# Loads of the values' matrices in the line of q and k, and three groups of early scores at other units, in a top-k attention with MLP

## The chip, the core and the metric

The kernel runs on one core of a Trainium2 chip. The metric is the device time of one execution in microseconds (us), as the median of several. A profile is one execution, recorded instruction by instruction; its span runs from the first instruction to the last.

Names: PE is TensorE (PEld its weight loads), DVE is VectorE, ACT is ScalarE, POOL is GpSimd, SP is SyncE, which issues every DMA of this kernel in the order of the program.

## The reference

Attention over 8 batches of 8 heads, 576 queries and keys, 64 dimensions a head, in float32. Of each row of scores the 32 largest are kept, and a softmax runs over them; then an MLP with 2048 hidden channels over the 4608 tokens.

```python
scores = scale * np.matmul(q, k.transpose(0, 1, 3, 2))
kth = np.partition(scores, -top_k, axis=-1)[..., -top_k:-top_k + 1]
scores = np.where(scores >= kth, scores, -1000000000.0)
attn = np.exp(scores - np.max(scores, axis=-1, keepdims=True))
attn = attn / (np.sum(attn, axis=-1, keepdims=True) + 1e-09)
x = np.matmul(attn, v)   # then (4608, 512), heads side by side
h = x @ w_in
out = np.maximum(0.01 * h, h) @ w_out
```

## The kernel before, in words

**Units.** Two heads form a pair: 32 pairs, four to a batch. A unit is 128 queries of a pair (or 64 queries of each of two pairs, for what is left of 576 = 4 x 128 + 64). There are 18 units to a batch, 144 in all, worked through one to a step: `cur = unit(s)` in step s. In even batches the 16 whole units come first and the two left ones last; in odd batches the left ones come first. So pairs 4 to 7 (batch 1) belong to units 18 to 35, pairs 8 to 11 to units 36 to 53, and so on.

**A unit's way.** Each step handles four units at different stages.

- Scores (`scores`, lines 203 to 237): in every even step PE computes the scores of units s + 2 and s + 3 as a pair into PSUM, and ACT copies them to SBUF (`s_sb`, line 235).
- Top-k of unit s (`top_k`): DVE runs four rounds of MAX8 (line 304) and MATCH_REPLACE8 (line 307) on larger and smaller halves (`pairs`, line 299).
- Unit s - 1: POOL masks (`pen`, lines 317 and 318), ACT takes exponents and their sums (line 321), then `ze` (line 326).
- Unit s - 2: DVE takes the reciprocals `rz` of `ze` (line 330), ACT normalizes (line 333). ACT then splits the words in two halves (`split`, line 342), each is written to DRAM (`apart`, line 343, 288 KB), and one transposing DMA reads both back (`wT`, line 347). Units 14, 15, 23 and 31 (`HASTY`) are transposed on PE instead (lines 357 and 363).
- Values: units n - 1 and n (n odd, from 15 on) are due together at the end of step n + 3 (`values_at`; one step earlier for n = 15, 23 and 31). There PE multiplies wT of the two units with the values' matrices `vt` (line 386, for left units line 398), and ACT copies the result to `x` (line 410).

**The MLP.** When all units of a chunk of 256 tokens have their values, its matmuls (`ph`, line 455, and `pz`, line 467) are dealt out in slots between these parts by a budget (`slot_budget`): the backlog spread over the slots up to the step that brings the next chunk.

**Loads.** q and k of a pair (`qt`, `kt`, eight pairs held, two 288 KB transfers a pair) wait in a list `waiting` and are issued one transfer a step, right after a unit's transposing DMA (line 671). The values' matrices (`vt`, five held, one 320 KB transfer a pair) are issued by `load_more` at the end of a step, as soon as the pair five before was last used four steps ago, several at once if they are due.

**Early scores.** The scores of twelve whole units are computed in steps 0 to 5 and put into DRAM (`keep_scores`, 576 KB a unit). `KEPT` names three groups a; a group is units a, a + 1, a + 8 and a + 9. Three steps ahead of its top-k such a unit's scores are fetched (`s_sb<-kept`, line 290, 576 KB), at the place where otherwise a transfer of the list goes. In the even step that would have computed the pair nothing is computed:

```python
            if unit(s + 3) in early_units:
                fetch_scores(unit(s + 3))
            elif waiting:
                nc.sync.dma_start(*waiting.pop(0))
...
            if new and new[0] in early_units:
                new = ()
```

The order within each engine is the order of the program; nothing is moved by a scheduler. In the functions below the line numbers are those of the profile.

Of the kernel before, what the change touches and what calls it, by code (L numbers as in the profile page):

```python
# [20 lines left out]
def kernel(  # L21
# [13 lines left out]
    nc = tc.nc  # L35
    NPAIR, P, S = qT.shape
# [20 lines left out]
    LOADED, LOADED_V = 5, 5  # L57
# [102 lines left out]
    qk_of, v_of = {}, {}  # L160

    def load_qk(pi, at_once=True):
        if pi % (LOADED + 3) < LOADED:
            qt = loads.tile([P, S], F32, name="qt")
            kt = loads.tile([P, S], F32, name="kt")
        else:
            raw = raws.tile([P, WCH, 4], U16, name="raw").rearrange("p n w -> p (n w)").bitcast(F32)
            qt, kt = raw[:, 0:S], raw[:, S:2 * S]
        waiting.extend([(qt, qT[pi]), (kt, kT[pi])])
        qk_of[pi] = qt, kt  # L170
        if at_once:
            while waiting:
                nc.sync.dma_start(*waiting.pop(0))

    waiting = []

    def load_v(pi):
        v_of[pi] = loads.tile([P, NKC, 2, D], F32, name="vt", bufs=LOADED_V)
        nc.sync.dma_start(v_of[pi], vk[pi])

    class Unit:

# [71 lines left out]
    def load_early(us):  # L254

        raw = raws.tile([P, WCH, 4], U16, name="raw").rearrange("p n w -> p (n w)").bitcast(F32)
        at = 0
        for pi in sorted({u.pairs[0] for u in us}):
            kt = raw[:, at:at + S]
            nc.sync.dma_start(kt, kT[pi])  # L260
            at += S
            for u in us:
                if u.pairs[0] == pi:
                    early_of[u] = raw[:, at:at + P], kt
                    nc.sync.dma_start(early_of[u][0], qT[pi][:, u.q0:u.q0 + P])
                    at += P
# [61 lines left out]
    def reciprocals(u):  # L328
        u.rz = small.tile([P, 2], F32, name="rz")
        nc.vector.reciprocal(u.rz, u.ze)  # L330
# [175 lines left out]
    LAG = 3  # L506
# [6 lines left out]
    def values_at(n):  # L513

        if n < UNHURRIED:
            return (n | 1) + LAG + 1, MIDDLE
        return (n | 1) + LAG - ((n | 1) in HURRIED), END

    steps = units

    KEPT = (24, 40, 56)
    EARLY_SCORES = {0: 4, 1: 2, 2: 1, 3: 2, 4: 1, 5: 2}

    def unit(n):
# [26 lines left out]

    with tc.manual_schedule():
        last = {p: n for n, u in enumerate(steps) for p in u.pairs}

        to_keep = [[steps[n] for n in (a, a + 1, a + 8, a + 9)] for a in KEPT]
        early_units = {u for us in to_keep for u in us}
        to_load, to_keep = list(to_keep), [u for us in to_keep for u in us]
        assert all(len(u.pairs) == 1 for u in to_keep)

        def score_early(count):  # L560

            for _ in range(min(count, len(to_keep))):
                keep_scores(to_keep.pop(0))
                if len(to_keep) % 4 == 0 and to_load:
                    load_early(to_load.pop(0))

        def load_more(s):

            for of, load, n, lag in ((v_of, load_v, LOADED_V, LAG + 1), (qk_of, load_qk, LOADED + 3, 8)):
                if of is qk_of and to_keep:  # L570
                    while len(of) < LOADED:
                        load(len(of))
                    continue
                while len(of) < NPAIR and (len(of) < n or last[len(of) - n] + lag <= s):
                    if of is v_of or len(of) < n:
                        load(len(of))
                    else:
                        if not waiting:
                            load(len(of), at_once=False)
                        break  # L580


        for n in range(3):
            load_weights(n)
        jobs = [round_weights(*job) for job in ROUNDED] if AS_WORDS else [iter(())] * len(ROUNDED)
        for n in range(len(jobs) + 1):
            if n == len(jobs) - 1:
                first = first_scores(steps[0])
                next(first, None)
            for job in jobs[max(n - 1, 0):n + 1][::-1]:  # L590
                next(job, None)
            if n == len(jobs) - 1:
                next(first, None)
                load_v(0)
                load_v(1)
            elif n == len(jobs):
                for _ in first_scores(steps[1]):
                    pass
            if n:
                load_weights(n + 2)  # L600
            if n >= len(jobs) - 2:
                load_early(to_load.pop(0))
            if 0 <= n - len(jobs) + HP + 1 < HP:
                load_qk(n - len(jobs) + HP + 1)

        def weights_of(u):
            reciprocals(u)
            normalize(u, 0)
            normalize(u, 1)

        def values(*place):
            due = [u for n, u in enumerate(steps) if values_at(n) == place]
            if not due:
                return ()
            po = ps_sc.tile([P, 2, 512], F32, name="wide", bufs=2)
            if len(due[0].pairs) == 1:
                weigh_whole(due, po, FULL + [NKC - 1] if place[1] == MIDDLE else
                            [QUARTERS] + FULL if place[0] < HURRY else FULL + [QUARTERS])
                return [(due[0], po[:, :, 0:P])]
            for n, u in enumerate(due):  # L620
                weigh_left(u, po[:, :, n * LEFT:(n + 1) * LEFT])
            return [(u, po[:, :, n * LEFT:(n + 1) * LEFT]) for n, u in enumerate(due)]

        def keep(weighed, *place):
            for u, po in weighed:
                keep_values(u.pairs[0], po, u.b, u.q0)
            attended(*place)

        for s in range(len(steps) + LAG + 1):
            assert s < 7 or not to_keep  # L630
            cur, old, older, new = unit(s), unit(s - 1), unit(s - 2), ()
            if s % 2 == 0:
                new = [u for u in steps[s + 2:s + 4] if u]
            picks = top_k(cur) if cur else iter(())
            budget = slot_budget(s)

            def slot():
                next(picks, None)

            at_first = s < HURRY and s - 2 in HURRIED  # L640
            if at_first:
                weights_of(older)
            slot()
            if old:
                mask(old, 0)
                mask(old, 1)
            late = s < HURRY and not {s - 1, s - 2} & set(HURRIED)
            if older and not late and not at_first:
                weights_of(older)
            mlp_steps(budget)  # L650
            weighed = values(s, MIDDLE)
            at_once = s - 2 in HASTY or any(at == (s, MIDDLE) for at, _ in ready_at)
            if at_once:
                keep(weighed, s, MIDDLE)
            slot()
            if older and late:
                weights_of(older)
            if s - 2 in HASTY:
                transpose_in_haste(older)
            mlp_steps(budget)  # L660
            if old:
                exponents(old, 0)
            mlp_steps(budget)
            if older:
                keep_transposed(older) if s - 2 in HASTY else transpose(older, lambda: mlp_steps(budget))
            if not older or s - 2 in HASTY:
                mlp_steps(budget)
            if unit(s + 3) in early_units:
                fetch_scores(unit(s + 3))
            elif waiting:  # L670
                nc.sync.dma_start(*waiting.pop(0))
            slot()
            slot()
            mlp_steps(budget)
            if old:
                exponents(old, 1)
                sums(old)
            mlp_steps(budget)
            if not at_once:
                keep(weighed, s, MIDDLE)  # L680
            if new and new[0] in early_units:
                new = ()
            if new and s < HURRY:
                scores(new)
            keep(values(s, END), s, END)
            if new and s >= HURRY:
                scores(new)
            score_early(EARLY_SCORES.get(s, 0))
            budget = slot_budget(s + 1)
            mlp_steps(budget)  # L690
            load_more(s)
        mlp_steps(1e9)

# [58 lines left out]
```

## Time and profile before

| | |
|---|---|
| median of 3 runs | 1460.74 us (1458.87 to 1461.27) |
| the profiled execution | 1460.92 us, of it span 1458.9 us |
| mean TensorE clock granted | 0.983 |
| PE busy | 1397.0 us, 96% of the span |
| PEld busy | 904.6 us, 62% |
| DVE busy | 1319.8 us, 90% |
| ACT busy | 1101.0 us, 75% |
| POOL busy | 1096.4 us, 75% |

The first top-k begins at 60.7 us, that of unit 143 at 1363.2 us. What follows after about 1384 us is MLP on PE. PE's busy time counts a matmul from its start to a modelled end, and overlapping ones once. A stage's PEclk is the share of the full TensorE clock that was granted. An engine's idle time is put down to what ended it ("<-"); a wait that does not hold up the end costs nothing.

### The profile page before, as it was taken

To read this page: it belongs to the slowest core of one execution; us is meant where nothing else is said; L and a number is where in the kernel's file an instruction comes from. 1 tells how busy PE (TensorE), PEld (TensorE's weight loads), DVE (VectorE), ACT (ScalarE), POOL (GpSimd) and SP (SyncE) were. 2 spreads that over 40 slices of the span, in tenths; PEclk is the share of its full clock that TensorE was granted. 3 is DMA by queue.
4 is the path that set the end of the run, shared out by engine and by line. 5 is a ranking of instruction groups with operands and counts; after the bars stand their busy time and mean duration, and the time that the engine had idled before them with its cause. 6 is when DMAs were issued, how large, how long until landed. Compare 5 with 4: busy or idle time off the path is not lost.

```text
span 1458.9 us, 26037 instructions
## 1 busy us (share of the span) xinstructions
PE 1397.0 (96%) x8978; PEld 904.6 (62%) x8980; DVE 1319.8 (90%) x3401; ACT 1101.0 (75%) x1984; POOL 1096.4 (75%) x744
## 2 busy tenths in 40 slices
PE   7848999899989999999999999999999999999998
PEld 2324548475656666666666666666666666666674
DVE  7999999989999999999999999999999999999600
ACT  8878888577767777778787878787878787778710
POOL 3388888878887888888888888888888888788600
PEclk9968999999999999999999999999999999999999
DMA  9967544647476676667666655557555665554610
GB/s 334 338 213 228 140 119 117 185 117 185 137 192 170 179 173 161 187 167 191 169 158 165 176 145 139 166 156 177 148 161 163 171 155 130 171 138 128 154 40 14
DMA packets 394996, 239.14 MB, mean 164 GB/s; under 512 B 334576, under 2 KB 336112, under 8 KB 392944
## 3 DMA queue, kind: packets, MB, share of 16 engines
q1 hardware_dynamic: 394864, 237.48, 58.7%
q8 instruction: 70, 1.15, 0.3%
q14 instruction: 62, 0.51, 0.1%
HBM read 55.77 MB, written 99.09 MB: 106 GB/s over the span
## 4 chain that ended last, share of the span: by engine, by line
PE 74%; DVE 12%; DMA 7%; ACT 5%; issue 1%; SPq 0%; POOL 0%; DVEq 0%; ACTq 0%; POOLq 0%
PE ph L455 28%; PE pz L467 28%; PE wide L386 9%; DVE tops L304 5%; PE wide L228 4%; DVE pairs L307 4%; DMA apart<-split 3%; PE narrow L228 3%; DMA wT<-apart 3%; ACT split L342 2%; DVE pairs L299 1%; PE wide L398 1%; ACT s_sb L321 1%; ACT s_sb L333 1%; DMA raw<-in_weights_dram 1%
## 5 line engine op out<-in xcount | busy, mean ns | idle before, releaser
L317 POOL TENSOR_SCALAR pen<-s_sb,tops 128x576 f32<-128x576 f32 x288 | 637.5, 2213 | 202.0 <-DVE tops L304 130.0
L304 DVE MAX8 tops<-pairs 128x8 f32<-128x288 f32 (+1 forms) x1152 | 636.0, 591 | 0.0
L467 PE MATMUL pz<-w_out,gT 128*128 128x512 f32 x1152 | 504.7, 594 | 2.4 <-ACT scale L428 2.4
L455 PE MATMUL ph<-x,w_in 128*128 128x256 f32 x2176 | 482.6, 381 | 0.0
L307 DVE MATCH_REPLACE8 pairs<-tops,pairs 128x288 f32<-128x288 f32 (+1 forms) x864 | 460.3, 538 | 0.0
L455 PEld LDWEIGHTS ph<-x,w_in 128*128 128x128 f32 x2176 | 409.5, 190 | 77.3 <-issue 23.1
L318 POOL TENSOR_TENSOR s_sb<-s_sb,pen 128x576 f32<-128x576 f32 x288 | 406.4, 1411 | 24.1
L467 PEld LDWEIGHTS pz<-w_out,gT 128*128 128x128 f32 x1152 | 216.4, 190 | 267.0 <-issue 261.5
L342 ACT COPY split<-s_sb 128x1152 uint16<-128x1152 uint16 x280 | 309.5, 1147 | 2.3 <-DMA apart<-split 2.2
L333 ACT ACTIVATE s_sb<-s_sb,rz 128x576 f32<-128x576 f32 x288 | 207.6, 773 | 36.9 <-DVE rz L330 36.6
L321 ACT ACTIVATE s_sb<-s_sb,nbias 128x576 f32<-128x576 f32 x288 | 222.3, 772 | 5.7 <-POOL s_sb L318 5.7
L299 DVE TENSOR_TENSOR pairs<-s_sb 128x576 f32<-128x576 f32 x288 | 213.6, 780 | 9.5
L386 PE MATMUL wide<-wT,vt 128*64 128x128 f32 (+1 forms) x2560 | 160.3, 284 | 14.5 <-DMA wT<-apart 10.9
L386 PEld LDWEIGHTS wide<-wT,vt 128*64 128x64 f32 (+1 forms) x2560 | 132.4, 139 | 63.8 <-issue 41.3
L410 ACT COPY x<-wide 128x128 f32<-128x128 f32 (+1 forms) x160 | 32.2, 260 | 130.9 <-PE wide L386 114.9
L461 ACT ACTIVATE gT<-ph 128x512 f32<-128x512 f32 x136 | 80.6, 593 | 56.1 <-PE ph L455 55.8
L235 ACT COPY s_sb<-wide 128x704 f32<-128x704 f32 x130 | 98.1, 755 | 9.4 <-PE wide L228 3.6
L476 ACT COPY o_sb<-pz 128x512 f32<-128x512 f32 x36 | 21.1, 585 | 90.3 <-PE pz L467 90.3
L228 PE MATMUL wide<-kt,qt 64*64 64x352 f32 x640 | 66.3, 476 | 1.0 <-ACT s_sb L250 0.7
L235 ACT COPY s_sb<-narrow 128x448 f32<-128x448 f32 x130 | 62.9, 536 | 0.9 <-PE narrow L228 0.4
L307 DVE MATCH_VALUE_LOAD pairs<-tops,pairs 128x8 f32 x864 | 62.7, 73 | 0.0
L330 DVE RECIPROCAL rz<-ze 128x2 f32<-128x2 f32 x144 | 22.2, 154 | 39.7 <-ACT ze L326 39.3
(69 smaller groups left out, 701.8 us busy)
## 6 DMA issues: line engine op xcount, KB each, us to landing
apart<-split SPq DMA_DIRECT2D x280, 288.0 KB, 2.3
raw<-in_weights_dram SPq DMA_DIRECT2D x15, 1024.0 KB, 7.1
vt<-in_vk_dram SPq DMA_DIRECT2D x32, 320.0 KB, 3.8
out_dram<-o_sb SPq DMA_DIRECT2D x36, 256.0 KB, 3.1
kept<-gT SPq DMA_DIRECT2D x12, 576.0 KB, 3.4
s_sb<-kept SPq DMA_DIRECT2D x12, 576.0 KB, 4.8
qt<-in_qT_dram SPq DMA_DIRECT2D x20, 288.0 KB, 3.5
kt<-in_kT_dram SPq DMA_DIRECT2D x20, 288.0 KB, 3.5
```

The lines of the kernel that those rows point to most:

```text
L228: nc.tensor.matmul(to[r0:r0 + LEFT, i, :], qt[d, q0:q0 + LEFT], kt[d, k0:k1], start=True, stop=True)
L299: nc.vector.tensor_tensor(pairs[:, :, n, :], u.both[:, :, 0:HS], u.both[:, :, HS:S], op)
L304: nc.vector.max(out=u.tops[:, i, r, :], in_=rest[i])
L307: nc.vector.match_replace(out=rest[i], in_to_replace=u.tops[:, i, r, :], in_values=rest[i], imm_value=LOWEST)
L317: nc.gpsimd.tensor_scalar(pen, u.s[i], u.tops[:, i, ROUNDS - 1, 7:8], MASKED, ALU.is_lt, ALU.mult)
L318: nc.gpsimd.tensor_tensor(u.s[i], u.s[i], pen, ALU.add)
L321: nc.scalar.activation(u.s[i], u.s[i], AF.Exp, bias=u.nbias[:, i:i + 1], scale=SCALE, accum_out=u.z[:, i:i + 1])
L333: nc.scalar.activation(u.s[i], u.s[i], AF.Copy, bias=0.0, scale=u.rz[:, i:i + 1])
L342: nc.scalar.copy(split, pairs[:, :, h])
L386: nc.tensor.matmul(po[n * D:(n + 1) * D, side, 0:P], v_of[u.pairs[0]][k, at, side, :], u.wT[k, at + side * NKC if at + 1 < NKC else at, :] ...
L455: nc.tensor.matmul(ph[:, i, 0:n], w_in[c][:, f * P:(f + 1) * P], x[c][:, 0:n], start=(c == 0), stop=(c == HP - 1),)
L467: nc.tensor.matmul(pz[0:m, 0:DMODEL], gT[:, f, r0:r0 + m], w_out[f // 4][:, f % 4, :], start=(f == 0), stop=(f == NFC - 1),)
```

## The change

The values' matrices get a list of their own, `waiting_v`. A buffer counts as free in the step whose values used it last (before: last unit's step plus four). A matrix whose first use lies more than two steps ahead goes into the list, and the line that issues a transfer of q or k a step takes from `waiting_v` first. Otherwise it is issued at the end of the step as before, at most two a step. The groups of early scores start at units 26, 62 and 98 where they were at 24, 40 and 56. The rest of the diff restates the loading of q and k without altering it, and guards a list.

```diff
-    waiting = []
-
-    def load_v(pi):
+    waiting, waiting_v = [], []
+
+    def load_v(pi, at_once=True):
         v_of[pi] = loads.tile([P, NKC, 2, D], F32, name="vt", bufs=LOADED_V)
-        nc.sync.dma_start(v_of[pi], vk[pi])
+        if at_once:
+            nc.sync.dma_start(v_of[pi], vk[pi])
+        else:
+            waiting_v.append((v_of[pi], vk[pi]))
+
+    def load_waiting():
+        if waiting_v or waiting:
+            nc.sync.dma_start(*(waiting_v or waiting).pop(0))
...
-    KEPT = (24, 40, 56)
+    KEPT = (26, 62, 98)
...
+        starts = {p: n for n, u in reversed(list(enumerate(steps))) for p in u.pairs}
...
-            for of, load, n, lag in ((v_of, load_v, LOADED_V, LAG + 1), (qk_of, load_qk, LOADED + 3, 8)):
-                if of is qk_of and to_keep:
-                    while len(of) < LOADED:
-                        load(len(of))
-                    continue
-                while len(of) < NPAIR and (len(of) < n or last[len(of) - n] + lag <= s):
-                    if of is v_of or len(of) < n:
-                        load(len(of))
-                    else:
-                        if not waiting:
-                            load(len(of), at_once=False)
-                        break
+            at_once = 2
+            while len(v_of) < NPAIR:
+                n = len(v_of)
+                due = values_at(starts[n])[0]
+                if n < LOADED_V:
+                    load_v(n)
+                elif values_at(last[n - LOADED_V])[0] > s:
+                    break
+                elif due > s + 2:
+                    load_v(n, at_once=False)
+                elif at_once:
+                    load_v(n)
+                    at_once -= 1
+                else:
+                    break
+            while len(qk_of) < NPAIR:
+                n = len(qk_of)
+                if n < LOADED or not to_keep and n < LOADED + 3:
+                    load_qk(n)
+                elif not to_keep and last[n - LOADED - 3] + 8 <= s and not waiting:
+                    load_qk(n, at_once=False)
+                else:
+                    break
...
-            if n >= len(jobs) - 2:
+            if n >= len(jobs) - 2 and to_load:
...
-            elif waiting:
-                nc.sync.dma_start(*waiting.pop(0))
+            else:
+                load_waiting()
```

## Prediction before the run

> **What bounds the kernel now.** I read the waits of all engines first, then the stages, then PE's order of time around PE's longest gaps. In the waits the columns are total us, times, longest.
>
> ```profile
> ACT x L410 <- PE wide L386: 114.9, 59, 5.3
> ...
> DVE rz L330 <- ACT ze L326: 39.3, 34, 6.6
> ...
> PE wide L386 <- DMA wT<-apart: 10.9, 6, 6.1
> ...
> PE wide L398 <- DMA vt<-in_vk_dram: 2.1, 1, 2.1
> ```
>
> A unit's top-k costs DVE 8.8 to 8.9 us without a break, and DVE's only stop from step 22 on is the reciprocal rz waiting for ze: 7.2 us in steps 22 to 41, 23.0 us from 441.5 to 1372. ze is late because ACT, working in order, waits for x: for PE to have made the values. So the loop is PE values, ACT copies x (and scores), normalizes, splits, then DMA apart, DMA transpose wT, and PE values again. The stages:
>
> ```profile
> 292.10:315.00 22.90, 22.89 (x144) 15.50 (x144) 17.81 (x47) 17.23 (x34) 14.99 (x11) 1.00 0.31 89
> ...
> 388.10:441.50 53.40, 45.93 (x302) 31.71 (x301) 52.89 (x138) 37.63 (x71) 44.92 (x31) 0.94 0.67 176
> ...
> 713.40:933.40 220.00, 220.00 (x1523) 146.79 (x1522) 212.19 (x553) 175.68 (x323) 179.59 (x121) 1.00 0.60 160
> ```
>
> The second number is PE, the fourth DVE. At 292 to 315 (steps 26, 27) DVE loses 5 us while PE is full; at 388 to 441 (steps 36 to 41) it is the reverse, PE has 7.5 us to spare; after 441 PE has hardly a gap. The Trainium skill (Perfetto Trace Analysis, Identifying the Most-Contended Engine) says that matmul busy time is a poor measure and that weight-load busy is the one to trust: 146.79 of 220, so a third of PE would be free and work moved off PE at steps 96 to 104 would bring nothing. The rows speak otherwise: 32 pz matmuls take 14.00 us at 269.67 and at 947.81 alike, back to back, and ACT waits for their end. I go by the rows; by the rule the last term of the sum below is 0.
>
> PE around its gaps, steps 22 to 25, then steps 39 and 40:
>
> ```profile
> 264.78 1.50 PE L398 MATMUL wide<-wT,vt 128*64 128x64 f32 x42
> 268.36 1.38 PE L398 MATMUL wide<-wT,vt 128*64 128x64 f32 x38 [2.08 <-DMA vt<-in_vk_dram]
> 269.67 14.00 PE L467 MATMUL pz<-w_out,gT 128*128 128x512 f32 x32
> 283.60 0.43 PE L386 MATMUL wide<-wT,vt 128*64 128x128 f32 x2
> 286.07 3.04 PE L386 MATMUL wide<-wT,vt 128*64 128x128 f32 x38 [2.04 <-DMA wT<-apart]
> 288.89 1.40 PE L228 MATMUL wide<-raw 64*64 64x352 f32 x8
> ...
> 291.90 1.98 PE L467 MATMUL pz<-w_out,gT 128*128 128x512 f32 x4
> ```
>
> ```profile
> 428.34 0.43 PE L386 MATMUL wide<-wT,vt 128*64 128x128 f32 x2
> 434.85 3.67 PE L386 MATMUL wide<-wT,vt 128*64 128x128 f32 x38 [6.08 <-DMA wT<-apart]
> 438.35 0.77 PE L228 MATMUL wide<-kt,qt 64*64 64x352 f32 x8
> ...
> 440.40 12.28 PE L467 MATMUL pz<-w_out,gT 128*128 128x512 f32 x28
> ```
>
> And why that last wT is late, on SP's queue:
>
> ```profile
> 423.15 0.57 SPq L290 DMA_DIRECT2D s_sb<-kept  x1
> 423.78 0.42 SPq L179 DMA_DIRECT2D vt<-in_vk_dram  x1
> 424.30 0.85 SPq L343 DMA_DIRECT2D apart<-split  x2
> 430.27 2.49 SPq L347 DMA_TRANSPOSE wT<-apart  x1
> ```
>
> A kept fetch and a values' matrix stand right ahead of the two apart transfers, and the transpose waits for both. Over the trace, an apart transfer with nothing issued in the 2 us ahead lands in 2.10 us (median of 206), behind one vt 3.8 (12), behind a fetch 5.0 (15), behind both 5.6 (4), behind a fetch and two vt 5.8.
>
> **What the change moves.** The order of the two programs shows DVE and POOL unchanged and PE with the same matmuls. (a) vt of pairs 8, 9 to 12, 16 and so on leave the ends of steps for the waiting line, one a step; their place on SP, between one step's transpose and the next step's apart, stays, so that alone is worth about 0. On SP a vt waits for the matmuls that last read its buffer, with the next apart queued behind it; those waits are 2.0 us in the whole trace, and a half step later they can only shrink. The edit counts where vt met fetches: in steps 20 to 22 and 36 to 39. (b) The six score pairs that are not computed in the loop move from steps 22, 30, 38, 46, 54, 62 to 24, 32, 60, 68, 96, 104; their fetches go to the step before and the step itself. A pair is PE 2.05 us (438.35 to 440.40) and ACT copies 0.75 + 0.97 + 0.77 = 2.49 us. What is computed early in steps 0 to 5, its loads and its stores keep number and size: 0, hidden as before under DVE, which those steps fill; bounded by nothing but placement in both directions.
>
> **Steps 22 to 27.** vt of pair 7 goes without a fetch and without a second vt: landed 3.8 us after about 262.0, at 265.8, before PE needs it (266.3). The wait of 2.08 goes; the scores of 24 and 25 come back at that place (2.05), so pz starts at about 269.7 as now. The apart transfers of units 20 and 21 no longer follow fetches: unit 20's transpose is issued about 3.5 us earlier, unit 21's wT lands at about 282 instead of 286.0, before PE comes at 283.7. The wait of 2.04 goes, and with it a half clock: PEclk was 0.50 from 287.43 to 290.85, the 38 matmuls took 3.04 instead of 2.35. The scores of 26 and 27 go (3.01 us, part at half clock). Together 2.04 + 0.69 + 3.01 = 5.7 us earlier at 291.90. Behind it stand DVE's stops of 2.26 (step 26) and 2.69 us (step 27), 4.95 in all. What is late next: nothing on PE; unit 22's wT, whose apart now follows the fetch of unit 26, lands by my count near 292, PE wants it at 295. ACT's 2.49 us of copies at step 22 bring ze of unit 22 to about 276.2, DVE wants it near 277. I take -4.9; ends -2.1 (only one wait gone) and -5.0.
>
> Here a rule is weighed. The Trainium skill (TensorE: Matmul & The Clock Gate, Why this matters for your kernels) warns only of gaps over about 3 us. In this trace the gap of 2.04 us was followed by 3.4 us of half clock, the gap of 6.08 by 6.8 us (430.79 to 437.62), the gap of 1.39 at 397 by none. By the rule the place is worth the gap and the pair at full clock, 2.04 + 2.05 = 4.1; by the rows 5.7, which covers both stops.
>
> **Steps 30 to 35.** A pair is added at 30 and taken at 32, PE is where it was at 365.1; a wait of 0.26 goes. About 0, ends -0.3 and +0.5 (ze of unit 30 comes within 0.1 us of DVE's need).
>
> **Steps 36 to 44.** At 38 the scores of 40 and 41 come back: PE reaches unit 37's values at 430.8 instead of 428.8. Its apart transfers start 2.5 us later (ACT copies first) but with one early vt and no fetch ahead; transpose at about 427.7, landed 432.2. The wait shrinks from 6.08 to about 1.4, too short for the half clock by the row at 397; the values end near 434.6 instead of 438.5, 3.8 us earlier. DVE's stops behind it are 2.22, 0.77 and 0.29 us (steps 42, 44, 46). I take -3.0; ends 0 and -3.3.
>
> **Steps 46 to 70.** Pairs come back at 46, 54 and 62 and go at 60 and 68: one pair more, +2.05, less two waits of PE (0.29 and 0.12) that it fills: +1.6. Ends 0 (room in steps 48 to 53, which show no stop) and +4.5 (three pairs at ACT's 2.49, less two at 1.5).
>
> **Steps 96 to 110.** Two pairs less. DVE's stops two and four steps on are 1.43, 0.41, 1.24 and 0.56 us: at most -3.6. The fetches put unit 95's and 103's apart at 5.0 us. How much of 2.05 then arrives is seen at step 46 now, with the same fetches: its relief lets the next values start 0.2 us after the next top-k, where at step 98, unrelieved, it is 1.6. So 1.4 to 1.8 each: -3.1; ends 0 and -3.6.
>
> Sum: -4.9 - 3.0 + 1.6 - 3.1 = -9.4. Counted from PE instead: waits gone 2.08 + 2.04 + 4.7 + 0.4 and half clock 0.7 + 1.0 + 1.3 make -12.2, less what PE then waits anew behind fetches, about 1: -11. The profiled execution took 1460.9 (span 1458.9 and 2.0 around it; the median is 0.2 below). 1460.9 - 9.4 = **1451.5 us**.
>
> **The rivals.** *Relief where the transfer sets the end.* Values start within 0 to 2 us of wT's landing all through the second half. If the fetch ahead of it takes all of what PE gains, steps 96 to 110 give 0; if at 42 to 46 PE's load after the values makes the stops, -1.0 is left there; in front only the stops' first, -2.3. Sum -2.3 - 1.0 + 1.6 = -1.7: 1459. For it: the 5.0 us. Against: step 46.
>
> *Slower: ACT's copies at 46, 54 and 62.* ACT copies scores ahead of the normalization that feeds wT. If this and not PE sets the loop, three pairs put back cost 3 x 2.49 = +7.5, the two taken at 60 and 68 fall on steps without a stop and give 0, front and middle give -2.3 - 1.0, the last part 0: +4.2, 1465. It decides if the values of 48 and 56 come later than about 1.6 us after the next top-k's start (now 0.2 and 0.1). Against it: ACT waits 114.9 us for PE's values and is busy 75%.
>
> That the change does not do what it says is excluded by the order: the fetches and vt stand where the code puts them.
>
> **Chances.** Forecast's case 0.76 (1446.5 to 1456.5), first rival 0.15, second 0.09. A difference of 0.2% (2.9 us) is about what can be told here: faster 0.76, same 0.15, slower 0.09. The range 1447 to 1459 leaves out the slower case, part of the first rival and a little below.
>
> **What would show it.** Right: no vt wait at 22, no wT wait at 24, PEclk 1.00 from step 8 to the tail, DVE's stops at steps 26, 27 and 42 gone, new ones at 50 to 60, those at 100 to 110 under 0.5. Wrong: wT waits of PE at 25, 62 or 98, or stops of over 1.5 us at 48 to 60 not given back by 78.

## The result, and the profile after

1455.65 us, median of 9 runs, against 1460.38 us for the kernel before on the same chip: the ratio is 0.9964, with an interval of 0.9953 to 0.9974, so about 5 us or 0.36% faster. About half of the forecast gain of 9.4 us came. The profiled execution took 1456.84 us, its span 1454.8 us. A second measurement on another chip gave 0.9975 (0.9966 to 0.9984). The kernel before took 1460.4, 1466.8, 1467.2 and 1460.8 us in the four measurements of this study, on different chips, so only ratios are compared below.

The waits of all engines, of the changed kernel (line numbers are 7 higher than before):

```profile
ACT x L417 <- PE wide L393: 111.9, 59, 4.1
...
DVE rz L337 <- ACT ze L333: 34.2, 29, 6.0
...
PE wide L393 <- DMA wT<-apart: 10.8, 10, 1.9
```

The wait for vt is gone, and PE's longest wait for wT fell from 6.1 to 1.9 us. But there are ten such waits where there were six, and their sum is as it was (10.9, now 10.8). What the change took away at the front came back elsewhere. The same three stages as before, by the units they hold:

```profile
294.10:311.90 17.80, 17.80 (x131) 13.60 (x129) 17.66 (x47) 13.46 (x25) 15.12 (x11) 1.00 0.41 122
382.70:436.10 53.40, 50.81 (x344) 33.30 (x343) 52.85 (x138) 44.15 (x81) 44.83 (x31) 1.00 0.61 165
706.60:927.70 221.10, 219.34 (x1521) 146.40 (x1520) 211.91 (x552) 175.03 (x323) 179.57 (x121) 1.00 0.58 159
```

Steps 26 and 27 take 17.8 us instead of 22.9, with DVE full. In steps 36 to 41 PE's idle time fell from 7.5 to 2.6 us, and PEclk is 1.00. In the third stage PE, which was busy for all of it, has 1.8 us of gaps.

PE in steps 22 to 25, and in steps 38 to 40:

```profile
266.81 2.55 PE L405 MATMUL wide<-wT,vt 128*64 128x64 f32 x80
269.29 0.82 PE L235 MATMUL wide<-kt,qt 64*64 64x352 f32 x8
...
271.39 14.00 PE L474 MATMUL pz<-w_out,gT 128*128 128x512 f32 x32
285.32 2.35 PE L393 MATMUL wide<-wT,vt 128*64 128x128 f32 x40
287.60 1.98 PE L474 MATMUL pz<-w_out,gT 128*128 128x512 f32 x4
```

```profile
424.83 0.43 PE L393 MATMUL wide<-wT,vt 128*64 128x128 f32 x2
426.34 2.34 PE L393 MATMUL wide<-wT,vt 128*64 128x128 f32 x38 [1.08 <-DMA wT<-apart]
428.50 0.77 PE L235 MATMUL wide<-kt,qt 64*64 64x352 f32 x8
```

Both waits of 2 us are gone, the scores of 24 and 25 stand at 269.29, and the half clock is gone. The 6.08 is 1.08, and 38 matmuls take 2.34 instead of 3.67.

Where the time went is read from DVE's order of time. I take the starts of the top-k of units 22, 36, 46 and so on, and compare the length of each stretch with the kernel before's profile (us; minus is shorter):

| stretch, units | predicted | changed kernel | again, other chip |
|---|---|---|---|
| 0 to 22 | 0 | +1.4 | +0.1 |
| 22 to 36 | -4.9 | -7.4 | -7.4 |
| 36 to 46 | -3.0 | -3.2 | -3.2 |
| 46 to 72 | +1.6 | +1.8 | +3.5 |
| 72 to 90 | 0 | +1.4 | +2.9 |
| 90 to 114 | -3.1 | -0.1 | 0.0 |
| 114 to 143 | 0 | +0.7 | +1.9 |

The first row is mostly one stop of DVE in step 8 (1.1 us before, 2.25 in one profile of the changed kernel, 1.18 in the other), which the change doesn't touch. The last column sets a profile from a chip on which the kernel before takes 1467.2 us against the kernel before's profile from one with 1460.4, so part of what it has more can be the chip's. The same holds for the stretches of the experiments below.

In the row that failed (90 to 114), SP's queue around the fetches of units 106 and 107 shows why, and PE the outcome:

```profile
1005.96 0.51 SPq L297 DMA_DIRECT2D s_sb<-kept  x1
1006.51 1.27 SPq L350 DMA_DIRECT2D apart<-split  x2
1012.50 2.84 SPq L354 DMA_TRANSPOSE wT<-apart  x1
1015.45 0.52 SPq L297 DMA_DIRECT2D s_sb<-kept  x1
1016.01 0.43 SPq L484 DMA_DIRECT2D out_dram<-o_sb  x1
1016.48 0.99 SPq L350 DMA_DIRECT2D apart<-split  x2
1023.86 2.62 SPq L354 DMA_TRANSPOSE wT<-apart  x1
```

```profile
1012.34 14.00 PE L474 MATMUL pz<-w_out,gT 128*128 128x512 f32 x32
1026.27 0.43 PE L393 MATMUL wide<-wT,vt 128*64 128x128 f32 x2
1028.62 2.34 PE L393 MATMUL wide<-wT,vt 128*64 128x128 f32 x38 [1.92 <-DMA wT<-apart]
```

From apart at 1016.48 to the transpose at 1023.86 SP waits 7.4 us for two transfers that stand behind a fetch and a store of the MLP's output (`out_dram`, 256 KB). No scores are computed between 1010 and 1026, so PE is early, and it waits 1.92 us for what the fetch has made late.

### The profile page after: what moved, and what is told of

It reads as the page before. It is cut to its first block, busy times and chain, and to the rows that moved or that the text cites. A ratio compares the mean times of both kernels' runs of the same rounds, so it can differ in the third digit from the quotient of the medians.

```text
span 1454.8 us, 26041 instructions
## 1 busy us (share of the span) xinstructions
PE 1395.0 (96%) x8980; PEld 902.3 (62%) x8980; DVE 1319.3 (91%) x3401; ACT 1100.8 (76%) x1984; POOL 1096.9 (75%) x744
## 4 chain that ended last, share of the span: by engine, by line
PE 82%; DVE 7%; DMA 5%; ACT 4%; issue 1%; POOL 0%; DVEq 0%; SPq 0%; ACTq 0%; POOLq 0%
PE pz L474 31%; PE ph L462 30%; PE wide L393 10%; PE wide L235 5%; DMA wT<-apart 3%; PE narrow L235 3%; DVE tops L311 2%; DVE pairs L314 2%; PE wide L405 1%; ACT split L349 1%; DMA raw<-in_weights_dram 1%; PE ph L430 1%; DMA apart<-split 1%; ACT s_sb L340 1%; ACT s_sb L328 1%
## 5 line engine op out<-in xcount | busy, mean ns | idle before, releaser
L393 PE MATMUL wide<-wT,vt 128*64 128x128 f32 (+1 forms) x2560 | 158.3, 282 | 15.6 <-DMA wT<-apart 10.8
L235 PE MATMUL wide<-kt,qt 64*64 64x352 f32 x704 | 73.2, 479 | 0.7 <-ACT s_sb L257 0.7
L328 ACT ACTIVATION_READ_ACCUMULATOR s_sb<-s_sb,nbias 128x1 f32 x288 | 55.3, 192 | 0.0
```

Of the source, the lines that this page charges most:

```text
L235: nc.tensor.matmul(to[r0:r0 + LEFT, i, :], qt[d, q0:q0 + LEFT], kt[d, k0:k1], start=True, stop=True)
L328: nc.scalar.activation(u.s[i], u.s[i], AF.Exp, bias=u.nbias[:, i:i + 1], scale=SCALE, accum_out=u.z[:, i:i + 1])
L393: nc.tensor.matmul(po[n * D:(n + 1) * D, side, 0:P], v_of[u.pairs[0]][k, at, side, :], u.wT[k, at + side * NKC if at + 1 < NKC else at, :] ...
```

## The experiments

Three theories at first. A: what counts is which transfers stand ahead of a unit's two apart transfers on SP's queue; the transposing DMA waits for these, and PE for it. Then the front gains because fetches and vt no longer stand there together, and the group at 98 gains nothing because its own fetches stand there. B: the waiting line of vt carries the gain. C, for the group at 98: PE's load or ACT's copies set the stops, not the fetches.

**The groups alone**, with vt loaded as before:

```diff
-    KEPT = (24, 40, 56)
+    KEPT = (26, 62, 98)
```

> The groups at 26, 62 and 98, with the values' matrices loaded as before (at the ends of steps, up to two at once). Theory A (transfers: the front and the middle gain because kept fetches no longer stand together with vt loads ahead of the same apart transfers, and the waiting line itself is worth nothing or costs a little at steps 73 to 83): 1453 to 1456, that is as fast as the changed kernel or up to 2 us faster, with DVE's stops at steps 26, 27 and 42 gone. Rival B (the waiting line of vt carries the gain): 1458 or more, with the vt wait or the stop at 42 still there.

The ratio to the kernel before is 0.9967 (0.9955 to 0.9978), as fast as the whole change. The stops at 26 and 27 are gone, that at 35 too; a stop of 2.23 us at step 38 is new and unexplained, the one at 42 is gone. B falls: the line is not needed for the gain.

**The line alone**, with the groups where they were:

```diff
-    KEPT = (26, 62, 98)
+    KEPT = (24, 40, 56)
```

> The values' matrices in the waiting line, with the groups still at 24, 40 and 56. Theory A: fetches take the line's place at steps 37 and 38, so the vt of pair 10 goes at step 40, the step that needs it; apart transfers behind fetches still at 5 us; the stops at 26 and 27 mostly stay: 1459 to 1462. Rival B: 1455 to 1457.

1.0049 (1.0035 to 1.0062), slower than before and worse than A expected. PE's waits in order of size:

```profile
PE wide L393 <- DMA vt<-in_vk_dram: 7.6, 2, 6.5
PE wide L393 <- DMA wT<-apart: 5.4, 8, 1.6
PE narrow L235 <- DMA raw<-in_kT_dram: 4.3, 1, 4.3
```

The wait of 6.5 us is the vt of pair 9, issued in step 40 at 430.8 us, right behind the fetches of units 40 and 41, and needed by the values of units 36 and 37 in that step. A had this for pair 10; in the run it was pair 9, and the vt of pair 11 cost another 1.1 us. Not foreseen: vt comes first in the line, so k came too late for the scores (4.3 us), once. The gaps brought half clock for 10.2 and 6.8 us. The two halves of the change depend on each other: with the groups at their old places the line costs 0.5%, with them at the new ones nothing that the ratios show.

**Two groups**, without the third:

```diff
-    KEPT = (26, 62, 98)
+    KEPT = (26, 62)
```

> The changed kernel with two groups only, at 26 and 62; the scores of units 98, 99, 106 and 107 are computed in the loop like the others. Theory A (the fetches ahead of apart take what the absent pairs give, so the group at 98 is worth 0 to 0.5 us): 1455 to 1456.5, within 1 us of the changed kernel, DVE's stops at 100 to 110 summing to about 3.6 us as in the kernel before. Rival C (the group does help by two pairs, about 3 us, and something else lost it): 1458 to 1459.

0.9942 (0.9927 to 0.9957). So the group at 98 not only gains nothing, the kernel is rather faster without it (the intervals of the two measurements of the changed kernel, 0.9953 to 0.9974 and 0.9966 to 0.9984, touch this one or lie above it). C, which asked for a slower kernel, falls. One part shows at the start: without the early scores of the third group, steps 0 to 22 are 1.0 us shorter than before, in this profile and in that of the other kernel with two groups below, and DVE's stop in step 8 (1.0 to 2.3 us in the kernels with three groups) is gone. The rest stays open; the spans (1457.6 us without, 1454.8 and 1457.2 with) come from different chips and cannot tell. Stops of DVE at steps 100 to 110: 4.7 us without the group, 4.1 and 4.2 with it; 3.6 before.

**The transfers at another place on the queue.** The step's fetch, or the transfer from the line, goes between the second apart and the transpose:

```diff
-    def transpose(u, between):
+    def transpose(u, between, load):
...
+        load()
         u.wT = work.tile([P, 2 * NKC - 1, P], F32, name="wT", bufs=3)
         nc.sync.dma_start_transpose(out=u.wT.bitcast(U16), in_=apart.rearrange("p h n -> (p h) n"))
...
+            def load():
+                if unit(s + 3) in early_units:
+                    fetch_scores(unit(s + 3))
+                else:
+                    load_waiting()
...
-            if unit(s + 3) in early_units:
-                fetch_scores(unit(s + 3))
-            else:
-                load_waiting()
```

(Where a unit is transposed on PE, `load()` is called at the old place.)

> The changed kernel with the step's fetch, or the transfer from the waiting line, issued between the second apart transfer and the transposing DMA instead of after the latter. SP waits there some 2 us for apart anyway, so the transfer runs in that time and no longer stands ahead of the next step's apart. Theory A (place in SP's queue takes the relief): PE's waits for wT at steps 62, 78, 98 and 106 shrink below 0.5, stops at 100 to 110 halve: 1450 to 1453. Rival C (copies on ACT or PE's load make the stops): 1454.5 to 1456.5. Rival D (the transpose, now behind a 576 KB transfer, lands later by more than it gains): over 1457.

0.9881 (0.9866 to 0.9896), and 0.9909 (0.9895 to 0.9923) when measured once more (below): 13 to 17 us faster than before, more than any theory had expected. In its profile the mean landing of an apart transfer is 2.36 us; in the changed kernel it was 2.78, before 2.81. PE's waits for wT at steps 62, 98 and 106 are gone, and DVE's stops at steps 100 to 110 sum to 1.1 us. D falls: with a fetch just ahead of it the transpose lands 5.0 us after its issue, with none 4.6 (medians; in the second run's profile 4.7 and 4.5).

**The same place in the kernel before**, **only the fetches at that place**, **two groups at that place**, and the changed kernel as it is:

```diff
             def load():
                 if unit(s + 3) in early_units:
                     fetch_scores(unit(s + 3))
-                else:
-                    load_waiting()
...
+            if unit(s + 3) not in early_units:
+                load_waiting()
```

(This is the second of them. The first moves `elif waiting: ...` of the old code in the same way, the third has `KEPT = (26, 62)`.)

> The kernel before (groups at 24, 40, 56, values' matrices at the ends of steps) with only the place on SP's queue altered: the fetch or the q or k transfer of a step goes between the second apart transfer and the transposing DMA. Theory A (what stands ahead of apart is the price): stops at 26, 27 and 42 shrink to about half, ratio to the kernel before 0.991 to 0.994, better than the change itself. Rival F (the place helps only together with the new groups): 0.997 to 1.0.

> The changed kernel with only the kept fetches at the new place; the waiting line of v, q and k stays behind the transposing DMA. Theory A with the fetches as the larger part (12 fetches of 576 KB, of which 4 are ahead of the group at 98): 0.990 to 0.993. Rival G (the 48 to 60 smaller transfers of the line carry most of it): 0.994 to 0.996.

> The kernel with fetches and line at the new place, but without the group at 98. Theory A (the group at 98 was worth nothing only because of its fetches, so at the new place it is worth two pairs): about 3 us slower than with three groups, 0.990 to 0.9915, stops at 100 to 110 at 3.6 us again against 1.1 with the group. Rival C (the group is worth nothing wherever its fetches stand): 0.988.

> The changed kernel once more, on the chip of the other three: 0.9955 to 0.9975 of the kernel before, as in its first measurement.

The place alone, without the change: 0.9914 (0.9899 to 0.9928), better than the change (F falls). Its DVE has no stop left at steps 26 to 30 and 42. Only the fetches: 0.9900 (0.9885 to 0.9916), so they are the larger part (G falls). Two groups: 0.9925 (0.9912 to 0.9938), slower than A allowed, against 0.9881 and 0.9909 with three (C falls). So now the third group is worth 0.2 to 0.4%, where at the old place it was worth nothing or less. In the profiles 2.6 us of it lie at units 90 to 114, as A has it; another 2.7 at units 114 to 134, where transfers with nothing ahead of them were slow (an apart of 4.26 us instead of 2.1, transposes of 5.3 and 5.4 instead of 4.5). That is not the chance of one execution: against the kernel before, this profile is 3.7 us longer there and the other one with two groups 3.0, those with three groups between -0.1 and +1.9. Each of these three slow transfers had a packet of program code beside it (last section); no run tested whether this is the cause. The changed kernel: 0.9975.

**The third group's fetches alone at the old place**, **a fourth group**, and the best kernel again:

```diff
+            def load():
+                if unit(s + 3) in early_units and s < 90:
+                    fetch_scores(unit(s + 3))
+                elif unit(s + 3) not in early_units:
+                    load_waiting()
...
+            if unit(s + 3) in early_units and s > 90:
+                fetch_scores(unit(s + 3))
```

```diff
-    KEPT = (26, 62, 98)
-    EARLY_SCORES = {0: 4, 1: 2, 2: 1, 3: 2, 4: 1, 5: 2}
+    KEPT = (26, 62, 98, 134)
+    EARLY_SCORES = {0: 4, 1: 2, 2: 2, 3: 2, 4: 2, 5: 2, 6: 2}
```

> The same kernel with three groups, but the four fetches of the group at 98 back behind the transposing DMA; everything else stays. Theory A (the place of just these four fetches decides what the group is worth): 2 to 4 us slower than with all at the new place, stops at 100 to 110 summing to about 3.5 instead of 1.1, waits of PE for wT at 98 and 106. Rival J (the place matters only for the crowded steps before 90): within 1 us of it.

> The kernel with fetches and line ahead of the transpose, and a fourth group at 134 (early scores two a step in steps 1 to 6). Theory A (at the new place a group is worth its two pairs where DVE stops): stops at 134 and 142 fall from about 4 us to under 1, 1 us is lost early: 2 to 3 us below the kernel with three groups. Rival H (the early steps have no room, or what lies behind step 130 is set by the tail): the same or up to 3 us slower.

> The kernel with fetches and line ahead of the transpose once more, on the same chip: 0.987 to 0.989 of the kernel before.

The third group's fetches behind the transpose: 0.9931 (0.9917 to 0.9945) against 0.9909, 2.8 us slower on the same chip, and no run of the one is as fast as the slowest of the other (1449.1 to 1452.7 us against 1446.8 to 1448.3). Four transfers differ in their place, and nothing else. J falls, and this is the cleanest evidence for A. SP's queue with the fetches ahead of the transpose, then behind it, at units 106 and 107:

```profile
1001.41 1.39 SPq L350 DMA_DIRECT2D apart<-split  x2
1002.90 0.38 SPq L297 DMA_DIRECT2D s_sb<-kept  x1
1004.87 2.42 SPq L355 DMA_TRANSPOSE wT<-apart  x1
```

```profile
1004.14 0.51 SPq L297 DMA_DIRECT2D s_sb<-kept  x1
1004.70 1.22 SPq L350 DMA_DIRECT2D apart<-split  x2
1010.62 3.18 SPq L355 DMA_TRANSPOSE wT<-apart  x1
```

From the first apart to the transpose it is 3.5 us in the one and 5.9 us in the other. DVE's stops in units 98 to 110 of the two:

```profile
DVE rz L337 <- ACT ze L333: 1.0, 3, 0.4
```

```profile
DVE rz L337 <- ACT ze L333: 3.6, 4, 2.1
```

The fourth group: 0.9982 (0.9975 to 0.9988), 11 us slower than three. A was right about the end (units 134 to 143 take 2.8 us less than with three groups) and wrong about the beginning: in steps 0 to 22 it loses 7.8 us more, with DVE stopping for 2.77 us in step 6 and 6.00 us in step 8. The early steps had no room for four more units, as H had it, though the loss is far over its 3 us. PE waits there for ACT to copy the early scores out of PSUM (up to 6.5 us at a time), but with three groups it does so too (up to 6.1), so which engine lacks the room is not shown. Another 2.9 us are lost at units 46 to 72, unexplained.

## Why the prediction was right, and where it was not

**What bounds the kernel** held: DVE stops nowhere but at rz (one 0.5 us stop apart), and PE's values set rz. Weight-load busy of 66% (146.40 of 221.10 us) did not mean that PE had a third free: with the transfers out of the way, moving two score pairs at steps 96 and 104 did shorten units 90 to 114, by 1.7 to 2.9 us in three profiles, where without the third group they took 0.3 more. The section that the prediction cites for it (the Trainium skill, Perfetto Trace Analysis, Identifying the Most-Contended Engine) names weight-load busy together with MFU, the matmul work against the peak, which the prediction left out.

**Steps 22 to 27**: right, both stops gone, -5 us as forecast. The stretch up to unit 36 gave 2.4 us more, mostly since the stops at 28, 30 and 35 (0.42, 0.40 and 1.22) went too; I had put steps 30 to 35 at about 0. The experiments point to the cause: the kernel before with the other place alone has these stops nearly gone as well (units 22 to 36: -6.7). The counted 5.7 us of PE are more than the two stops, and the rest carried on to the next. The weighing of the clock rule came out for the rows: without the gap of 2 us the half clock went as well, though such a gap brings it in some executions only (last section).

**Steps 36 to 44**: right in mechanism and size (-3.2 for -3.0; the wait 1.08 for 1.4, and no half clock).

**Steps 46 to 70**: +1.8 and +3.5 for +1.6, but not for the reason given. I charged score pairs. With the same pairs at the same steps and only the transfers moved, the stretch is +0.6 and +0.3; with the fetches alone moved it is +1.6, on the chip that gave +3.5. So most of the loss is fetches ahead of apart at steps 59, 60, 67 and 68: PE waits for wT 1.09 us at step 62 and 0.60 at 70.

**Steps 72 to 90**: I had no term for it, and it cost +1.4 and +2.9. Most of that is a stop of DVE in step 80 (1.22 and 1.54 us, none before), behind PE's wait for the wT of unit 75 (1.76 and 2.07 us). The line is a suspect, since in steps 73 to 78 it sends vt and q one at a time ahead of apart. But with only the fetches moved, and the line where the change has it, the wait is short and the stretch -0.5. The changed kernel, then the one with only the fetches moved:

```profile
772.67 2.34 PE L393 MATMUL wide<-wT,vt 128*64 128x128 f32 x38 [1.76 <-DMA wT<-apart]
```

```profile
768.58 2.34 PE L394 MATMUL wide<-wT,vt 128*64 128x128 f32 x38 [0.60 <-DMA wT<-apart]
```

The apart transfers of unit 75 landed in 2.1 us in both. What was late is the transpose itself: 6.6 us from issue to landing in the changed kernel (6.9 in its second profile), 5.5 with the fetches moved, where 4.5 is usual. While it was under way (766.02 to 772.62 us) the changed kernel's DMA queues show, beside the kernel's own transfers, two packets of program code (packets, MB, share of the DMA engines' time):

```profile
q14 instruction: 1, 0.01, 1.7%
q8 instruction: 1, 0.02, 1.1%
```

With two groups no such packet falls there, the transpose lands in 4.6 us and PE does not wait. The last section counts this over all profiles. So the sentence that the line's place alone "is worth about 0" stands: the groups without the line gave 0.9967, with it 0.9964 and 0.9975.

**Steps 96 to 110**: the step that failed. "How much of 2.05 then arrives is seen at step 46 now, with the same fetches" gave -3.1; measured -0.1 and 0.0. At step 46 I had read how early the values began and not what the fetches had cost in the steps around; and the values of 98 and 106 wait for the very units (95 and 103) whose apart stands behind the last fetch. This is the first rival's mechanism, in the place it named. Its "against: step 46" was worth less than its "for it: the 5.0 us".

**The slower rival**, ACT's copies at 46, 54 and 62, did not come: with all transfers at the new place those steps lose 0.3 to 0.6 us. The sign that I had named for it did show at step 56, whose values begin 1.94 us after the next top-k. But they do so in the fastest kernel too (1.95), so the sign does not tell this rival from the others.

**The total** is near the forecast partly by luck: the 2.4 us at units 28 to 36, which I had put at 0, make up for some of the 3.1 that did not come at 96 to 110.

## What to carry to other kernels

On a queue that issues in order and waits, look at what stands ahead of the transfer that the next wait is for, not at how busy the DMA engines are: a bulk load belongs into the time in which the queue waits for something anyway (here between the last store and the transposing load that depends on it). There 576 KB made the load land 0.1 to 0.5 us later; ahead of the stores they made each of these land 2.9 us later. When work is taken off the engine that sets the pace, price the transfer that brings its replacement first; if it feeds the same wait, it can take all of the gain. Two edits that share one slot a step have to be run apart, since one alone can be worse than neither.

## What the runs showed of the hardware

- Half clock after short gaps is not regular. Gaps of PE of 2.04 us (before), 2.09 us (two groups) and 1.80 us (groups alone) were followed by 3.4 us at half clock; gaps of 2.08 us (before), 1.92 us (changed kernel), 2.07 us (its second profile) and 2.21 us (the place alone) were not. A gap of 2.14 us near 193 us, which all 13 profiles of this study have, was followed by it in five of them.
- A transposing DMA lands in 4.5 to 4.7 us with nothing issued shortly ahead, and in 4.6 to 5.1 with a 576 KB read issued some 2 us ahead (medians of the profiles with the fetches at the new place). A 288 KB write behind the same read takes 5.0 us instead of 2.1.
- Single transfers are slow with nothing issued close ahead: in the changed kernel 20 of 209 apart transfers took over 3 us (median 2.09). Where such a one falls on the path, PE waits for it (1.1 to 1.8 us at units 117 to 127 in four of the profiles). The places are not random: the transpose of unit 62 took over 5.2 us in 11 of the 13 profiles, those of units 70, 82 and 132 in the two with two groups and in no other.
- The slow ones go together with the loading of program code, which the profile lists as DMA queues of kind `instruction`. Of the 286 transposes of all 13 profiles that took over 5.2 us, 277 had a code packet of 8 or 16 KB under way between issue and landing, of the other 1534 only 530. Of the 183 apart transfers that took over 3 us with nothing issued in the 2 us ahead, 173 had one, of the other 2867 only 477. That is an association: no run moved the code packets alone.
